# Subtraction, product and low half of the second softmax moved from GpSimd to VectorE for batches 1 to 7

## Chip, cores and metric

The kernel runs on one core of a Trainium2 chip. The core has five engines that run side by side and wait for each other by semaphores: TensorE (PE for its matmuls, PEld for its weight loads), VectorE (DVE), ScalarE (ACT), GpSimd (POOL) and SyncE (SP, which here issues the DMAs). The metric is device time in microseconds (us) of one execution. Lower is better.

## Reference

Two attentions with a softmax each, then two feed-forward layers. Shapes: batch B = 8, heads H = 8, sequence S = 576, head size 64, 32 packed rows; the layers have 4608 tokens, width 512 and inner width 2048. Weights come in 64-bit floats.

```python
def sm_attn(qq, kk, vv):
    s = scale * np.matmul(qq, kk.transpose(0, 1, 3, 2))
    s = s - np.max(s, axis=-1, keepdims=True)
    a = np.exp(s)
    a = a / (np.sum(a, axis=-1, keepdims=True) + 1e-09)
    return np.matmul(a, vv)
p_packed = sm_attn(p, k, v)             # first softmax, over 576
x = sm_attn(q, p_packed, p_packed)      # second softmax, over 32
x = x.transpose(0, 2, 1, 3).reshape(B * S, H * D)
h = x @ moe_w_in;  x = (h - np.tanh(h)) @ moe_w_out
h = x @ moe2_w_in; out = (h * np.cos(h)) @ moe2_w_out
```

## The kernel before, in words

**High and low halves.** A product is formed from a rounded high half and the rest, the low half: each operand t is split into h (ScalarE copies t to fp32r) and l = t - h, and three products h*h, l*h, h*l are summed in PSUM. The splits that this case touches are a2 (the second softmax's weights; L429 writes the high half, L430 the low half), g (L493, L498) and the layer's activations (gh on L561, gl on L565).

**Layer 1.** The last product of the second attention is never formed on its own: `gmat` multiplies the packed rows by the weights w1i (tile gp, L479), and `h1` (L517) multiplies the result g by the softmax weights a2. Work goes in 128 steps, `for n, (blk, s) in enumerate(steps)`. Each step makes one pair of h blocks with 12 matmuls of 128x288, works on it elementwise, and multiplies the activations of the step before last by w1o (`ymm1`, L578, 16 matmuls with gh and 8 with gl, into tile y). Per step the chain is: PE h; ACT t and u (L532, L533); DVE t, d, y, and the masked copy (L544, L545, L546, L550); ACT gh (L561); POOL gl (L565); PE y. L545 is the last that reads h from PSUM. On POOL a one-element memset (L556) of tile d stands ahead of gl, so that gl starts with L550 and not earlier.

**PSUM.** Pool `psh` has two tiles. All of these take turns in them: h of each step, the scores sc and s2, the transposes tp and pt, pp, and gp. A tile is taken again when its last reader is done: L545 for h, the second L498 for gp.

**Attention of batch b.** `attention(b, half)` queues 12 pieces, for two halves of the heads, into lists `early[n]` and `mid[n]`, which the steps n empty. For b >= 2 it starts at step at = 16 (b - 1); the second softmax of half 0 has s2 at step at+8, `s2m` at the end of at+8, `s2e` at the end of at+9, `s2n` at the end of at+10, `s2t` at the end of at+11, and `s2h` early in at+12, ahead of that step's L544. Half 1 is two steps later. So the ends of steps at+10 to at+14 and the starts of at+12 and at+14 hold the pieces in question; steps at+9, at+11, at+13 and at+15 hold gp and its two L498. The weights a2 are first used at step at+16. For b = 1 the pieces lie in steps 1 to 11, and its a2 are first used by h of step 8. Batch 0 comes ahead of the steps.

**Order.** From step 15 on the order of each engine's instructions is that of the code (`manual_schedule`). Steps 0 to 14 are ordered by the framework's scheduler, which places instructions by its own costs; there the engine of an instruction changes the order of others too.

After layer 1 comes layer 2 (from about 772 us), which uses none of the changed lines.

Of the kernel before, what the change touches and what calls it, by code (L numbers as in the profile page):

```python
# [78 lines left out]
def fused_kernel(ctx, tc, qT, kT, v, pT, w1i, w1o, w2i, w2o, ident, out):  # L79
    nc = tc.nc  # L80
# [241 lines left out]

    def attention(b, half, at=None, tsc=0, ttr=0, tpp=0, ts2=0):
        x = {}
        eng = nc.vector if b == 0 else nc.gpsimd

        def sc():
            k = ld.pop(("k", b, half))
# [645 lines left out]
    for x in LOADS.split():  # L974
# [6 lines left out]
        else:  # L981
            load0_qk(x[0], {"k": kT, "q": qT}[x[0]], int(x[1]))
    SCO, EX, RC, TR, PP, PX, S2, S2M, S2E, S2N, S2T, S2H = range(12)
    A0, A1 = (attention(0, half) for half in range(2))
    with tc.manual_schedule():
        for fn in (
# [20 lines left out]
    for b in range(1, B):  # L1007
        at = 16 * (b - 1)
        at_pair(at + (PACK1 if b == 1 else PACK), ppack, ppack2, b)
        for c in range(4):  # L1010
            at_pair(at + (G1 if b == 1 else G)[c], gmat, gsplit, b, c)
            if b > 1:
                mid[at + G[c] - 2].append(lambda c=c: load_w1(c))
        for half in range(2):
            attention(b, half, at, *(ATT1 if b == 1 else ATT)[half])
        lk0, lk1, lv0, lv1, lq0, lq1 = LOAD1 if b == 1 else LOAD
        mid[at - 4].append(lambda b=b: load_p(b))
        mid[at + lk0].append(lambda b=b: load_qk("k", kT, b, 0))
        mid[at + lk1].append(lambda b=b: load_qk("k", kT, b, 1))
        mid[at + lv0].append(lambda b=b: load_v(b, 0))  # L1020
        mid[at + lv1].append(lambda b=b: load_v(b, 1))
        mid[at + lq0].append(lambda b=b: load_qk("q", qT, b, 0))
        mid[at + lq1].append(lambda b=b: load_qk("q", qT, b, 1))
# [518 lines left out]
```

## Time and profile before

| | us |
|---|---|
| median of 3 runs (1494.94 to 1496.75) | 1496.19 |
| the profiled execution | 1494.03 |
| its span, first to last instruction | 1492.2 |
| PE, DVE, ACT, POOL busy | 1440.5, 1184.2, 1034.6, 383.8 |
| layer 1, steps 17 to 113, in the trace | about 153 to 700 |

The profiled execution is 2.2 us below the median of the three. Busy times of engines overlap each other; that an engine is busy doesn't say that anything waits for it.

### The profile page before, as it was taken

To read this page: it belongs to the slowest core of one execution; us is meant where nothing else is said; L and a number is where in the kernel's file an instruction comes from. 1 tells how busy PE (TensorE), PEld (TensorE's weight loads), DVE (VectorE), ACT (ScalarE), POOL (GpSimd) and SP (SyncE) were. 2 spreads that over 40 slices of the span, in tenths; PEclk is the share of its full clock that TensorE was granted. 3 is DMA by queue.
4 is the path that set the end of the run, shared out by engine and by line. 5 is a ranking of instruction groups with operands and counts; after the bars stand their busy time and mean duration, and the time that the engine had idled before them with its cause. 6 is when DMAs were issued, how large, how long until landed. Compare 5 with 4: busy or idle time off the path is not lost.

```text
span 1492.2 us, 29411 instructions
## 1 busy us (share of the span) xinstructions
PE 1440.5 (97%) x11296; PEld 1305.9 (88%) x11296; DVE 1184.2 (79%) x1562; ACT 1034.6 (69%) x1592; POOL 383.8 (26%) x356
## 2 busy tenths in 40 slices
PE   4789999999999999999999999999999999999998
PEld 2578999989998899988998888998889988998898
DVE  6998787777878788789976778886888688868874
ACT  5899767879788787977875656655665466636652
POOL 0353454554645455454550000000000000000000
PEclk8799999999999999999999999999999999999999
DMA  9642464646647474564669757776668766776656
GB/s 356 217 159 75 144 207 139 226 143 207 211 170 246 159 246 150 198 216 151 196 244 382 247 165 231 231 254 211 206 186 255 220 203 192 237 237 205 182 161 186
DMA packets 179980, 307.67 MB, mean 206 GB/s; under 512 B 14912, under 2 KB 110144, under 8 KB 179840
## 3 DMA queue, kind: packets, MB, share of 16 engines
q1 hardware_dynamic: 179840, 305.79, 62.8%
q8 instruction: 90, 1.47, 0.4%
q14 instruction: 50, 0.41, 0.1%
HBM read 238.35 MB, written 67.37 MB: 205 GB/s over the span
## 4 chain that ended last, share of the span: by engine, by line
PE 77%; ACT 8%; DVE 5%; issue 5%; POOL 3%; DMA 1%; SPq 0%; DVEq 0%; POOLq 0%; ACTq 0%
PE p L899 21%; PE y L578 17%; PE y L909 15%; PE h L517 9%; PE p L909 6%; PE h L639 3%; PE y L715 3%; POOL gl L565 2%; PE gp L479 2%; DVE y L550 1%; ACT u L533 1%; ACT st L175 1%; ACT st L170 1%; ACT y L539 1%; DVE y L546 1%
## 5 line engine op out<-in xcount | busy, mean ns | idle before, releaser
L899 PE MATMUL p<-b,hw 128*128 128x512 f32 x1302 | 310.4, 391 | 0.0
L578 PE MATMUL y<-gh,w1o 128*128 128x288 f32 x2048 | 305.3, 301 | 3.2 <-DVE ye L608 1.0
L578 PEld LDWEIGHTS y<-gh,w1o 128*128 128x128 f32 x2048 | 279.1, 189 | 31.1 <-issue 12.0
L899 PEld LDWEIGHTS p<-b,hw 128*128 128x128 f32 x1302 | 239.1, 188 | 47.0
L565 POOL TENSOR_TENSOR gl<-y,gh 128x576 fp32r<-128x576 f32 x127 | 245.7, 1935 | 22.4 <-ACT gh L561 22.4
L517 PE MATMUL h<-a,g 128*128 128x288 f32 x1536 | 228.8, 298 | 17.8 <-DVE d L545 7.6
L517 PEld LDWEIGHTS h<-a,g 128*128 128x128 f32 x1536 | 212.9, 190 | 21.7 <-ACT st L170 8.2
L532 ACT ACTIVATE t<-h 128x576 f32<-128x576 f32 x128 | 85.3, 667 | 122.9 <-PE h L517 122.8
L578 PE MATMUL y<-gl,w1o 128*128 128x288 f32 x1024 | 157.6, 296 | 5.5 <-POOL gl L565 5.2
L578 PEld LDWEIGHTS y<-gl,w1o 128*128 128x128 f32 x1024 | 142.7, 188 | 9.2 <-POOL gl L565 8.7
L550 DVE COPY_PREDICATED y<-k,t 128x576 f32<-128x576 int16 x128 | 132.4, 1035 | 9.9
L909 PE MATMUL y<-yw,yh 128*128 128x256 f32 x768 | 136.2, 279 | 0.2 <-DMA yw<-wod 0.2
L544 DVE TENSOR_TENSOR t<-h,t 128x576 f32<-128x576 f32 x128 | 95.2, 744 | 51.2 <-ACT u L533 50.7
L909 PEld LDWEIGHTS y<-yw,yh 128*128 128x128 f32 x768 | 117.6, 188 | 0.9 <-ACT o L920 0.4
L546 DVE SCALAR_TENSOR_TENSOR y<-y,d 128x576 f32<-128x576 f32 x128 | 104.0, 813 | 16.9 <-ACT y L539 10.4
L909 PE MATMUL y<-yw,yl 128*128 128x256 f32 x384 | 107.4, 280 | 0.0
L917 DVE TENSOR_TENSOR yl<-k,yh 128x1024 fp32r<-128x1024 f32 x72 | 87.1, 1220 | 23.4 <-ACT yh L920 22.9
L561 ACT ACTIVATE gh<-y 128x576 fp32r<-128x576 f32 x128 | 88.2, 689 | 9.9 <-DVE y L550 9.6
L545 DVE TENSOR_TENSOR d<-u,h 128x576 f32<-128x576 f32 x128 | 94.9, 742 | 0.0
L909 PE MATMUL y<-yw,gh 128*128 128x256 f32 x512 | 94.0, 280 | 0.0
L909 PE MATMUL p<-yw,yh 128*128 128x256 f32 x512 | 91.0, 279 | 0.0
L920 ACT ACTIVATE c<-p 128x512 f32<-128x512 f32 x96 | 56.9, 593 | 47.7 <-PE p L899 47.7
(166 smaller groups left out, 2609.1 us busy)
## 6 DMA issues: line engine op xcount, KB each, us to landing
yw<-wso SPq DMA_DIRECT2D x128, 256.0 KB, 3.0
hw<-wsi SPq DMA_DIRECT2D x124, 256.0 KB, 3.0
w1i<-w1d SPq DMA_DIRECT2D x48, 512.0 KB, 5.2
yw<-wod SPq DMA_DIRECT2D x96, 256.0 KB, 3.3
hw<-wid SPq DMA_DIRECT2D x93, 256.0 KB, 3.2
y<-ye SPq DMA_DIRECT2D x80, 144.0 KB, 1.9
st<-w1i SPq DMA_DIRECT2D x16, 512.0 KB, 8.4
v<-vv SPq DMA_DIRECT2D x16, 512.0 KB, 6.7
```

Source lines behind the costliest of these rows:

```text
L517: nc.tensor.matmul(out=h[:, x, 0:HB], lhsT=gw[b, f // 4, half][:, ga, c0:c0 + 128], rhs=a2[b, half][:, aa, HB * j:HB * j + HB], start=(n = ...
L532: nc.scalar.activation(out=st["t"], in_=h, func=AF.Tanh)
L544: lambda: nc.vector.tensor_tensor(out=t, in0=hs, in1=t, op=ALU.subtract),
L545: lambda: nc.vector.tensor_tensor(out=d, in0=u, in1=hs, op=ALU.mult),
L546: lambda: nc.vector.scalar_tensor_tensor(out=y, in0=y, scalar=PC0 - PC1 * PC1 / (4 * PC2), in1=d, op0=ALU.add, op1=ALU.mult,),
L550: lambda: nc.vector.copy_predicated(out=y, mask=k.bitcast(I16), data=t),
L561: nc.scalar.activation(out=st["gh"], in_=st["g"], func=AF.Copy)
L565: eng.tensor_tensor(out=st["gl"], in0=st["g"], in1=f32(st["gh"]), op=ALU.subtract)
L578: nc.tensor.matmul(out=yps[blk][d][:, 0:HB], lhsT=w1out[f][:, wh, 128 * d:128 * d + 128], rhs=st[gg][:, x, :], start=(s in first and x == ...
L899: nc.tensor.matmul(out=dst, lhsT=w[:, wi, 128 * j:128 * j + 128], rhs=b[j][bi], start=(first and n == 0), stop=(n == 5), skip_group_check= ...
L909: nc.tensor.matmul(out=dst[m // 2][:, 256 * (m % 2):256 * (m % 2) + 256], lhsT=src[:, 128 * m:128 * m + 128], rhs=w[:, wi, :], start=(firs ...
L917: nc.vector.tensor_tensor(out=out, in0=x, in1=y, op=op)
```

## The change

One line of `attention`: the engine of three instructions. Before, they ran on VectorE for batch 0 and on GpSimd for batches 1 to 7; now they run on VectorE for all.

```diff
     def attention(b, half, at=None, tsc=0, ttr=0, tpp=0, ts2=0):
         x = {}
-        eng = nc.vector if b == 0 else nc.gpsimd
+        eng = nc.vector
...
         def s2m():
...
             eng.tensor_tensor(
                 out=x["u3"], in0=x["u3"], in1=m.to_broadcast([128, NG, 32]), op=ALU.subtract
             )
...
         def s2n():
...
             eng.tensor_tensor(
                 out=x["u3"], in0=x["u3"], in1=r.to_broadcast([128, NG, 32]), op=ALU.mult
             )
...
         def s2h():
...
             eng.tensor_tensor(
                 out=t[:, 1, :], in0=x["ut"], in1=f32(t[:, 0, :]), op=ALU.subtract
             )
```

That is L407, L419 and L430, 128x576 each, in two halves of seven batches: 42 instructions. POOL keeps gl (L565), its memset, and the low halves of the weights (L232).

**Steps 42 and 43** (batch 3, as in batches 2 to 7), VectorE: the end of step 42 up to the first reads of h of step 43.

```order
 L417 TENSOR_SCALAR r<-r 128x18
 L418 RECIPROCAL r<-r 128x18
+L419 TENSOR_TENSOR u<-u,r 128x576
 L406 TENSOR_REDUCE m<-u 128x18
+L407 TENSOR_TENSOR u<-u,m 128x576
 L544 TENSOR_TENSOR t<-h,t 128x576
 L545 TENSOR_TENSOR d<-u,h 128x576
```

Two instructions now stand between L418 and L544.

**Step 44**, VectorE: the end of step 43 (g, then the transpose ut of half 0) and the start of step 44; `a_4070` is a2 of half 0 of batch 3.

```order
 L498 TENSOR_TENSOR g<-gp,g 128x512 x2
 L425 STREAM_TRANSPOSE ut<-u 128x576
+L430 TENSOR_TENSOR a_4070<-ut,a_4070 128x576
 L544 TENSOR_TENSOR t<-h,t 128x576
 L545 TENSOR_TENSOR d<-u,h 128x576
```

L430 reads what ScalarE's L429 writes, and L544 of step 44 now stands behind it. The end of step 44 (L418, L419, then L544 of step 45) has one more, and step 46 has L430 of half 1 ahead of its L544.

**The scheduled part, batch 1**, VectorE before: `a` isn't in these rows, since its low half is made on POOL; ut is that of half 1, and the L498 are those of the first gp of batch 1.

```order
118 L425 STREAM_TRANSPOSE ut<-u 128x576
119 L546 SCALAR_TENSOR_TENSOR y<-y,d 128x576
120 L208 SCALAR_TENSOR_TENSOR wt<-wt,st 128x512
121 L550 COPY_PREDICATED y<-k,t 128x576
122 L498 TENSOR_TENSOR g<-gp,g 128x512 x2
```

And now (`a_1145` is a2 of half 1 of batch 1):

```order
123 L498 TENSOR_TENSOR g<-gp,g 128x512
124 L550 COPY_PREDICATED y<-k,t 128x576
125 L498 TENSOR_TENSOR g<-gp,g 128x512
126 L425 STREAM_TRANSPOSE ut<-u 128x576
127 L208 SCALAR_TENSOR_TENSOR wt<-wt,st 128x512
128 L187 SCALAR_TENSOR_TENSOR st<-st 128x512
129 L208 SCALAR_TENSOR_TENSOR w1i<-w1i,st 128x512
130 L430 TENSOR_TENSOR a_1145<-ut,a_1145 128x576
```

The transpose has moved from ahead of the L498 to behind them, and three instructions of the weights' conversion stand between it and L430.

## Rows read from the trace of the kernel before

**Rows 1.** Busy us by stretch (PE, PEld, DVE, ACT, POOL), clock, DMA: scheduled part's end, then steps 17 to 113.
```profile
75.00:153.00 78.00, 69.91 (x642) 62.95 (x641) 69.69 (x95) 72.88 (x129) 36.37 (x37) 1.00 0.34 119
153.00:700.00 547.00, 539.41 (x5234) 500.17 (x5234) 438.47 (x672) 428.63 (x756) 285.21 (x259) 1.00 0.55 188
```

**Rows 2.** Waits of PE, 153 to 700 us: total us, times, longest.
```profile
PE h L517 <- DVE d L545: 2.3, 4, 0.7
PE y L578 <- POOL gl L565: 1.7, 3, 0.8
```

**Rows 3.** By source line: duration ns min/median/max, first and last start us.
```profile
L407 POOL TENSOR_TENSOR u<-u,m x14: 1153/1160/1687, 76.8 to 662.4; 128x576 f32<-128x576 f32 x14
L407 DVE TENSOR_TENSOR u<-u,m x2: 757/758/759, 20.6 to 22.9; 128x576 f32<-128x576 f32 x2
L417 DVE TENSOR_SCALAR r<-r x16: 158/618/627, 26.7 to 672.0; 128x18 f32<-128x18 f32 x16
L550 DVE COPY_PREDICATED y<-k,t x128: 795/830/2092, 46.8 to 769.5; 128x576 f32<-128x576 int16 x128
```

**Rows 4.** Timeline, steps 42 to 46: start us, us, instruction, [idle before, releaser].
```profile
301.57 0.70 DVE L406 TENSOR_REDUCE m<-u 128x18 f32<-128x576 f32 x1
302.25 0.76 DVE L544 TENSOR_TENSOR t<-h,t 128x576 f32<-128x576 f32 x1
302.92 0.74 DVE L545 TENSOR_TENSOR d<-u,h 128x576 f32<-128x576 f32 x1
...
305.23 1.76 PE L517 MATMUL h<-a,g 128*128 128x288 f32 x12
...
306.64 0.77 DVE L425 STREAM_TRANSPOSE ut<-u 128x576 f32<-128x576 f32 x1
308.11 0.69 ACT L429 ACTIVATE a<-ut 128x576 fp32r<-128x576 f32 x1
308.26 0.76 DVE L544 TENSOR_TENSOR t<-h,t 128x576 f32<-128x576 f32 x1 [0.85 <-ACT u L533]
...
309.98 0.96 DVE L546 SCALAR_TENSOR_TENSOR y<-y,d 128x576 f32<-128x576 f32 x1 [0.30 <-ACT y L539]
...
311.09 2.02 POOL L565 TENSOR_TENSOR gl<-y,gh 128x576 fp32r<-128x576 f32 x1
...
312.52 0.63 DVE L417 TENSOR_SCALAR r<-r 128x18 f32<-128x18 f32 x1
...
313.37 0.69 DVE L544 TENSOR_TENSOR t<-h,t 128x576 f32<-128x576 f32 x1
...
316.01 1.23 PE L517 MATMUL h<-a,g 128*128 128x288 f32 x8
```

**Rows 5.** Timeline, steps 78 to 80 of batch 5.
```profile
498.43 1.27 DVE L498 TENSOR_TENSOR g<-gp,g 128x512 fp32r<-128x512 f32 x2
...
500.15 1.76 PE L517 MATMUL h<-a,g 128*128 128x288 f32 x12
500.31 0.71 DVE L544 TENSOR_TENSOR t<-h,t 128x576 f32<-128x576 f32 x1
...
501.84 1.09 PE L479 MATMUL gp<-w1i,pt 64*32 64x256 f32 x32
...
509.15 0.72 PE L317 MATMUL sc<-k,pin 64*32 64x288 f32 x16 [0.76 <-PE h L517]
```

**Rows 6.** Timeline, step 30 of batch 2.
```profile
229.37 2.36 PE L578 MATMUL y<-gh,w1o 128*128 128x288 f32 x16 [1.05 <-DVE ye L608]
```

**Rows 7.** Timeline, scheduled part, around h of step 8, the first that needs a2 of batch 1.
```profile
92.90 1.82 POOL L430 TENSOR_TENSOR a<-ut,a 128x576 fp32r<-128x576 f32 x1
93.34 2.07 DVE L550 COPY_PREDICATED y<-k,t 128x576 f32<-128x576 int16 x1
...
99.50 0.40 PE L517 MATMUL h<-a,g 128*128 128x288 f32 x1 [2.13 <-ACT g L493]
...
102.09 1.19 PE L517 MATMUL h<-a,g 128*128 128x288 f32 x7 [0.17 <-POOL a L430]
```

## Prediction

> **What bounds the kernel now.** I read the busy times by stretch first [rows 1]. In steps 17 to 113, where 36 of the 42 moved pieces lie, PE is busy 539.4 of 547 us and VectorE 438.5: PE is the bound, and VectorE has 108 us idle. In the last 78 us of the scheduled part, where the six pieces of batch 1 lie, ScalarE is fullest (72.9 of 78), with PE and VectorE (69.9, 69.7) close behind. Then the waits of PE [rows 2]: from 153 to 700 us it waited 2.3 us for L545, four times, and 1.7 us for POOL's gl. So POOL costs PE next to nothing there, and taking work off it can give back 1.7 us at most. Then the timeline around one batch's pieces [rows 4], to see how late VectorE may be before PE waits. L545 of step 43 ends at 302.92 + 0.74 = 303.66, 1.41 us after its L544 began, and leaves its PSUM tile to h of step 44, which starts at 305.23: 1.57 us later. L544 of step 45 begins at 313.37, so its L545 ends at about 314.78 and h of step 46, which takes that tile, starts at 316.01: 1.23 us later. These two intervals, less some 0.1 us that a hand-over takes (my choice), are all the room there is.
>
> **The change, part by part.** A piece takes 0.76 us on VectorE (batch 0's, with POOL quiet) and took 1.16 on POOL [rows 3]. 36 pieces are 27 us, which would fit into 108 us of idle time if they stood where it is. They don't.
>
> *A shared resource.* L417 is a tiny instruction: 158 ns at the least, 618 at the median [rows 3]. In step 44 it starts at 312.52, beside gl (311.09 + 2.02 = 313.11), and ends at 313.15 [rows 4]: it was held until POOL was done. The Trainium skill, "SBUF — State Buffer", section "Who interferes with whom", has the rule: a Vector instruction with two SBUF inputs and a GpSimd instruction that reads SBUF exclude each other, and the later one waits for the whole of the earlier. By that rule alone each batch's first piece would cost its wait as well, and the sum below would be some 3 us higher. What the rows say of it: L407 of half 0, at the end of step at+8, comes beside a gl as that L417 does, and would be held some 0.5 us. I price it at nothing all the same: it is followed by an L544 that waits for ScalarE's u, as most of the L544 do, and by 1.5 us of room like that of step 43. If that cover were gone, it would cost up to 0.76 + 0.5 us in six batches, 8 us. The other five pieces of a batch come behind a finished gl, or while POOL waits, and run at 0.76.
>
> *Batch 3, step by step* [rows 4].
> - End of step 42: L419 and L407 in front of L544 of step 43, which started right behind L406 (301.57 + 0.70). It is late by 2 x 0.76 = 1.5 us. The room at step 44 is 1.57 - 0.1: PE loses 0 to 0.1.
> - Step 44: L425 is 1.5 us late too and ends at 308.9; ScalarE's L429 (0.69) waits for it instead of running at 308.11, and ends at 309.65; L430 follows, 0.76; L544 behind it starts at 310.4 instead of 308.26, 2.1 late. VectorE's idle 0.85 us ahead of that L544 is used up.
> - End of step 44: L546 had waited 0.30 us and taken 0.96 (beside POOL's L430; 0.76 otherwise), so the copy L550 and gl are 1.7 late, not 2.1. gl ends at 314.8, L417 is held until then, L418 and L419 follow: L544 of step 45 is 1.7 + 0.8 = 2.5 late, at 315.9, its L545 ends at 317.3, and h of step 46 starts at 317.4 instead of 316.01. **PE loses 1.4 us.**
> - Step 46: L430 of half 1 makes its L544 late again, but the next taker of that tile, gp of step 47, stands behind the 12 matmuls of another h. I take 0.
>
> Batches 4 and 6 repeat this: 3 x 1.4 = **4.2 us**.
>
> *Batches 5 and 7* have a long low half (128x1024, of the combined weights) at the end of steps 77 and 109. The two L498 behind it ended at 499.70 and end 2.2 us later (2.5 less the waits ahead of L546), at 501.9; h of step 79 takes their tile and started at 500.15, now 501.55: it loses 0.45 more. L425, L429 and L430 follow, so L544 of step 78 moves from 500.31 to about 501.85 + 0.77 + 0.69 + 0.76 + 0.1 = 504.1: 3.8 late. gp of step 79 takes that tile and started 0.1 us after its L545 (500.31 + 1.41 against 501.84), so PE is 3.8 late as well. At sc of step 80, where PE waited 0.76 us for a tile, 0.7 comes back [rows 5]. 3.1 each, **6.2 us**.
>
> *Batch 2.* PE already waits 1.05 us in step 30 for L608 [rows 6], four evacuations that stand behind L419, two L498 and L425 on VectorE. There is no room: they come as late as VectorE is at that point, 2.5 as in batch 3 and 0.4 more because VectorE waits less for u in step 28. **2.9 us**.
>
> *Batch 1, scheduled.* Most of h of step 8 started at 102.09, when POOL's L430 of half 1 was done [rows 7]. On VectorE this L430 now comes behind five other pieces and three conversions that stood elsewhere (the third pair of orders): 6 x 0.76 + 3 x 0.7 = 6.6 us more work ahead of it. Against this: L550 at 93.34 took 2.07 us beside POOL's L430 instead of 0.83 [rows 3, 7], 1.2 back; the piece itself is 0.7 shorter than its 1.46 on POOL (my estimate from the gap between 100.59, where ScalarE released it, and 102.05); and PE does about 0.9 us of y and gp ahead. That leaves 3.8. ScalarE, the fullest engine here, gets no work, so some of it comes back from later waits: I take **3 us**. Bounds: -2.1, if all of PE's idle time ahead of that h (2.13) went, and +6.6.
>
> *Sum.* 4.2 + 6.2 + 2.9 + 3 = 16.3. The profiled execution took 1494.0 and would take 1510.3; the median of the runs lies 2.2 above it, so about **1512 us**.
>
> **Rivals.** What a measurement of this kernel can tell from no change is about 0.2%, 3 us.
>
> *The room is enough (no change).* For it: VectorE is busy only 80% of the stretch, and the room is 1.57 and 1.23 us against pieces of 0.76. It would hold if the lateness did not pile up over steps 42 to 45, that is, if VectorE caught up in step 44. Against it: 0.85 + 0.30 + 0.2 us is all that it can catch up there, and three pieces are 2.3, with L429 in between. Batch 2 and the scheduled part would have to cancel too. 1496 us, within 3.
>
> *Faster: the softmax chain was POOL's.* "GPSIMD Engine Reference", Engine selection, in the Trainium skill, puts elementwise work on VectorE and calls GpSimd about two times slower with two inputs. The trace has 1.16 against 0.76 us [rows 3], 1.5 times. As a mechanism here: the chain to a2 of batch 1 gets 0.4 to 0.7 us shorter in each of its three pieces, h of step 8 no longer waits (2.13), and PE's waits for gl (1.7) go. That is 3.8 us, 1492. It decides if the last L425 of batch 1 is not held up behind the L498, and if nothing is lost in the steps at+13; the order shows the first to be otherwise.
>
> *VectorE becomes the bound around the pieces.* If each piece costs PE its whole 0.76 (27 us) and the scheduled part 6.6, it is 1494 + 34 + 2 = 1530. For it: three pieces in a row already leave no idle time. Against it: L407 of half 0 and L430 of half 1 have room.
>
> *The change does not do what it says:* excluded, since the order shows all 42 on VectorE.
>
> **How the numbers follow.** My forecast, slower by 6 to 25 us: 0.79. VectorE as the bound, above that: 0.05. A part of the terms covered, slower by 3 to 6 us: 0.04. Room enough: 0.07. Faster: 0.05. So slower 0.88, same 0.07, faster 0.05. The range: the steady term could be 1 to 1.5 times the three certain stalls (about 9 to 18 us), and the scheduled part -2 to 6.6; not all at one end: 1502 to 1521.
>
> **What would show it.** L407, L419, L430 on VectorE at 0.76, and at most the first of each batch longer. PE waiting for L545 some 1.4 us at the h of steps 46, 62 and 94; 1.4, 0.5 and 1.8 at the h, h and gp of steps 78 to 79, and the like at 110 to 111; the wait for L608 in step 30 grown from 1.05, together with that for L545 at its h, by 2.9. POOL some 50 us less busy and VectorE 25 to 30 more. h of step 8 some 3 to 4 us later. The prediction is wrong if L544 of step 45 is less than 1.2 us late, or if step 16 begins earlier than before, or if gl itself becomes late for PE.

## Result: slower by 1.1%, and the profile after

| | before | after |
|---|---|---|
| median of 5 runs each, us | 1496.01 (1494.94 to 1496.75) | 1511.79 (1510.35 to 1513.99) |
| ratio | 1 | 1.0113 [1.0103, 1.0124] |
| profiled execution, us (its span) | 1494.03 (1492.2) | 1513.38 (1511.6) |

The medians differ by 15.8 us, the two profiled executions by 19.4: that of before lies 2.0 under its median and that of after 1.6 above. Part of these 3.6 us is the clock of TensorE, told below; that it is all of them isn't shown.

Busy time of the changed kernel, from the page:

```profile
PE 1445.8 (96%) x11296; PEld 1309.1 (87%) x11296; DVE 1213.2 (80%) x1604; ACT 1038.0 (69%) x1592; POOL 330.5 (22%) x314
```

Busy us by stretch, the end of the scheduled part and steps 17 to 113, with the clock granted to PE after the engines (compare [rows 1]):

```profile
75.00:158.00 83.00, 71.02 (x639) 63.68 (x638) 73.68 (x100) 73.24 (x129) 28.63 (x31) 0.98 0.31 110
158.00:720.00 562.00, 544.31 (x5238) 503.06 (x5237) 463.58 (x709) 432.29 (x756) 240.10 (x223) 1.00 0.54 183
```

Steps 17 to 113 take about 562 us instead of 547 (14.8 us more up to step 120, by the starts of h). GpSimd has lost 45 us of work there and VectorE has gained 25, but VectorE still has 98 us idle. So these 15 us are no lack of time on VectorE. The waits of PE in that stretch (total us, times, longest; compare [rows 2]):

```profile
PE h L517 <- DVE d L545: 8.5, 12, 1.0
PE gp L479 <- issue: 3.3, 2, 1.6
PE y L578 <- DVE ye L608: 2.1, 1, 2.1
PE sc L317 <- PE h L517: 2.1, 4, 0.6
PE y L578 <- POOL gl L565: 0.7, 1, 0.7
```

PE waits for L545 three times as often. The two "issue" waits at gp are also waits for a PSUM tile that L545 had not left (below). The moved pieces themselves, by source line (duration ns min/median/max; compare [rows 3]):

```profile
L407 DVE TENSOR_TENSOR u<-u,m x16: 745/760/1200, 20.9 to 680.1; 128x576 f32<-128x576 f32 x16
L419 DVE TENSOR_TENSOR u<-u,r x16: 739/758/760, 27.4 to 692.1; 128x576 f32<-128x576 f32 x16
L430 DVE TENSOR_TENSOR a<-ut,a x16: 734/758/762, 31.7 to 700.9; 128x576 fp32r<-128x576 f32 x16
```

They take 0.76 us at the median, as forecast; some L407 take up to 1.20. Batch 3, timeline of steps 43 to 45 (compare [rows 4]; h of step 42 begins 10.03 us later than before):

```profile
313.18 0.76 DVE L407 TENSOR_TENSOR u<-u,m 128x576 f32<-128x576 f32 x1
313.85 0.75 DVE L544 TENSOR_TENSOR t<-h,t 128x576 f32<-128x576 f32 x1
...
318.13 0.77 DVE L425 STREAM_TRANSPOSE ut<-u 128x576 f32<-128x576 f32 x1
318.93 0.69 ACT L429 ACTIVATE a<-ut 128x576 fp32r<-128x576 f32 x1 [0.45 <-DVE ut L425]
...
319.64 0.76 DVE L430 TENSOR_TENSOR a<-ut,a 128x576 fp32r<-128x576 f32 x1 [0.75 <-ACT a L429]
...
320.32 0.75 DVE L544 TENSOR_TENSOR t<-h,t 128x576 f32<-128x576 f32 x1
...
325.82 0.75 DVE L544 TENSOR_TENSOR t<-h,t 128x576 f32<-128x576 f32 x1
```

Take 10.03 us off each L544 and compare with 302.25, 308.26 and 313.37: they are 1.6, 2.0 and 2.4 us late (forecast 1.5, 2.1, 2.5). Between them L429 waits for the late L425, and L430 waits 0.75 us for L429 while L544 stands behind it.

Batch 5, steps 78 and 79 (compare [rows 5]; h of step 76 begins 13.3 us later than before):

```profile
515.06 1.84 PE L517 MATMUL h<-a,g 128*128 128x288 f32 x12 [0.31 <-DVE g L498]
515.64 0.69 ACT L429 ACTIVATE a<-ut 128x576 fp32r<-128x576 f32 x1 [2.82 <-DVE ut L425]
516.35 0.76 DVE L430 TENSOR_TENSOR a<-ut,a 128x576 fp32r<-128x576 f32 x1 [0.75 <-ACT a L429]
517.03 0.75 DVE L544 TENSOR_TENSOR t<-h,t 128x576 f32<-128x576 f32 x1
...
518.54 1.10 PE L479 MATMUL gp<-w1i,pt 64*32 64x256 f32 x32 [1.64 <-issue]
```

gp starts 0.1 us after the end of the L545 behind that L544: that is what "issue" hides. It is 16.7 us later than before, so 3.4 us were lost since step 76 (forecast 0.45 + 1.4 + 1.8 = 3.65 up to there, of which 0.7 comes back).

### The profile page after: what moved, and what is told of

Same layout as the page of the kernel before. It is cut to its first block, busy times and chain, and to the rows that moved or that the text cites. A ratio compares the mean times of both kernels' runs of the same rounds, so it can differ in the third digit from the quotient of the medians.

```text
span 1511.6 us, 29391 instructions
## 1 busy us (share of the span) xinstructions
PE 1445.8 (96%) x11296; PEld 1309.1 (87%) x11296; DVE 1213.2 (80%) x1604; ACT 1038.0 (69%) x1592; POOL 330.5 (22%) x314
## 4 chain that ended last, share of the span: by engine, by line
PE 77%; DVE 8%; ACT 7%; issue 5%; POOL 2%; DMA 1%; SPq 0%; DVEq 0%; ACTq 0%; POOLq 0%
PE p L899 20%; PE y L578 17%; PE y L909 15%; PE h L517 10%; PE p L909 6%; PE h L639 3%; PE y L715 3%; DVE y L550 2%; PE gp L479 1%; POOL gl L565 1%; DVE t L544 1%; DVE d L545 1%; ACT u L533 1%; ACT st L175 1%; DVE y L546 1%
## 5 line engine op out<-in xcount | busy, mean ns | idle before, releaser
L565 POOL TENSOR_TENSOR gl<-y,gh 128x576 fp32r<-128x576 f32 x127 | 246.4, 1940 | 30.5 <-ACT gh L561 30.2
L517 PEld LDWEIGHTS h<-a,g 128*128 128x128 f32 x1536 | 213.5, 190 | 33.1 <-PE y L578 13.9
L550 DVE COPY_PREDICATED y<-k,t 128x576 f32<-128x576 int16 x128 | 131.0, 1023 | 9.9 <-ACT k L542 0.2
L544 DVE TENSOR_TENSOR t<-h,t 128x576 f32<-128x576 f32 x128 | 95.6, 747 | 37.6 <-ACT u L533 36.8
L546 DVE SCALAR_TENSOR_TENSOR y<-y,d 128x576 f32<-128x576 f32 x128 | 99.8, 780 | 15.8 <-ACT y L539 8.5
L561 ACT ACTIVATE gh<-y 128x576 fp32r<-128x576 f32 x128 | 88.1, 688 | 15.1 <-DVE y L550 14.8
L545 DVE TENSOR_TENSOR d<-u,h 128x576 f32<-128x576 f32 x128 | 94.9, 742 | 0.0
L556 POOL MEMSET d<- 128x1 f32 x127 | 12.6, 99 | 363.7 <-DVE y L546 353.2
L539 ACT ACTIVATE y<-u 128x576 f32<-128x576 f32 x128 | 87.4, 683 | 6.5 <-POOL gl L565 6.0
```

The costliest lines, as they stand in the source:

```text
L517: nc.tensor.matmul(out=h[:, x, 0:HB], lhsT=gw[b, f // 4, half][:, ga, c0:c0 + 128], rhs=a2[b, half][:, aa, HB * j:HB * j + HB], start=(n = ...
L539: nc.scalar.activation(out=y, in_=u, func=AF.Square, scale=PC2 ** 0.5, bias=PC1 / (2 * PC2 ** 0.5))
L544: lambda: nc.vector.tensor_tensor(out=t, in0=hs, in1=t, op=ALU.subtract),
L545: lambda: nc.vector.tensor_tensor(out=d, in0=u, in1=hs, op=ALU.mult),
L546: lambda: nc.vector.scalar_tensor_tensor(out=y, in0=y, scalar=PC0 - PC1 * PC1 / (4 * PC2), in1=d, op0=ALU.add, op1=ALU.mult,),
L550: lambda: nc.vector.copy_predicated(out=y, mask=k.bitcast(I16), data=t),
```

## Experiments

Each kernel ran on one chip beside the kernel before, not all on the same chip; "ratio" is against that kernel there, with its 95% interval. The table shows how many us each stretch of the program grew against the profiled execution of before, from the starts of the first weight load of h in steps 8, 17, 34, 50, 66, 82, 98 and 120.

| kernel | ratio | batch 1 | 2 | 3 | 4 | 5 | 6 | 7 |
|---|---|---|---|---|---|---|---|---|
| changed | 1.0113 [1.0103, 1.0124] | 5.5 | 4.6 | 1.4 | 1.5 | 3.2 | 1.4 | 2.8 |
| changed, again | 1.0110 [1.0096, 1.0124] | 6.6 | 2.9 | 1.4 | 1.5 | 3.2 | 1.4 | 3.0 |
| batch 1 only | 1.0026 [1.0017, 1.0035] | 4.1 | 0.0 | 0.0 | 0.0 | 0.0 | 0.0 | 0.0 |
| batches 2 to 7 | 1.0120 [1.0106, 1.0133] | 0.9 | 2.9 | 2.3 | 1.5 | 3.2 | 1.5 | 3.2 |
| low half only | 1.0040 [1.0028, 1.0053] | 1.0 | 0.9 | 0.0 | 0.0 | 1.4 | 0.1 | 1.2 |
| subtraction, product | 1.0076 [1.0063, 1.0089] | 0.0 | 3.6 | 1.4 | 0.6 | 1.5 | 0.6 | 2.0 |
| low half late | 1.0075 [1.0063, 1.0088] | 1.1 | 4.1 | 0.8 | 0.8 | 2.6 | 0.8 | 2.8 |
| first subtraction | 1.0000 [0.9992, 1.0009] | 1.0 | 0.0 | 0.0 | 0.0 | 0.2 | 0.6 | 0.0 |
| changed, L608 first | 1.0114 [1.0099, 1.0130] | 4.1 | 6.6 | 1.4 | 1.4 | 3.1 | 1.8 | 2.9 |
| the same, stores kept | 1.0104 [1.0089, 1.0120] | 6.5 | 3.7 | 1.4 | 1.4 | 3.1 | 1.8 | 3.0 |
| before, L608 first | 1.0002 [0.9993, 1.0011] | 1.0 | 0.1 | 0.0 | 0.0 | 0.1 | 0.0 | 0.0 |
| low half twice | 1.0088 [1.0074, 1.0102] | 0.8 | 1.6 | 1.3 | 1.3 | 4.3 | 1.3 | 3.9 |
| batch 1: four pieces | 1.0009 [1.0000, 1.0018] | 4.2 | 0.1 | 0.0 | 0.0 | 0.1 | 0.0 | 0.0 |

**Batch 1 only.**

```diff
-        eng = nc.vector
+        eng = nc.vector if b < 2 else nc.gpsimd
```

> The six pieces of batch 1 alone (with those of batch 0, which were there before) on VectorE; GpSimd keeps the 36 of batches 2 to 7. Theory (late turns of the two-tile PSUM pool, and a longer chain to the low half of batch 1's a2): step 17 begins 5.5 us later than before, as in the changed kernel, nothing is added after it, and the h of steps 46, 62, 94 and the gp of steps 79 and 111 wait as before; median 1500 to 1502. Rival 1 (each piece costs the same share of the 15.8 us): 6 of 42 pieces, 2.3 us, 1498.3. Rival 2 (the steps written by hand hold the whole loss): 1496.

Step 17 begins 3.7 us later (it grew 4.1 from step 8 on, which began 0.4 early), and nothing is added behind it. The median, 1498.57, is under the 1500 to 1502 that I expected. It is 3.7 us above before's 1494.82 and so above both rivals, the nearer one only just (its interval is 2.5 to 5.2, that rival at 2.3). It stays 1.8 us under the 5.5 of the changed kernel, with the same order on PE. Most of that is the clock: behind the wait for L429, from 104.86 us to the start of the last matmuls of h, 4 matmuls of h, 12 of gp and 5 of y took 3.5 us there, at 0.50 from about 105 us on, and 2.1 in this kernel at 1.00. This kernel's clock fell as well, from 99.0 to 102.4 us, but ahead of a wait for L429 (1.12 us).

**Batches 2 to 7.**

```diff
-        eng = nc.vector
+        eng = nc.gpsimd if b == 1 else nc.vector
```

> All 36 pieces of batches 2 to 7 on VectorE, those of batch 1 on GpSimd as before. Theory: steps 0 to 16 as before; then batch 2 +4.3, batches 3, 4 and 6 +1.4 each, 5 and 7 +2.8 each as in the changed kernel, 14 us in the trace by step 127; median 1506 to 1509. The two parts add up: this and the kernel with batch 1 alone together make the 15.8 us. Rival (the parts hide each other, or GpSimd's relief in batch 1 pays for some of it): the sum of the two differs from 15.8 by more than 2 us.

Batch by batch it loses what the changed kernel loses, batch 2 even the forecast 2.9. The median is 1512.16, 3 us above what was expected, and by medians the two parts sum to 0.26 + 1.20 = 1.46%, where the whole has 1.10 to 1.13; by the profiled spans they sum to 3.1 + 15.4 = 18.5 us against 19.4. So GpSimd's relief pays for nothing: a sum that misses the whole by more than 2 us was the rival's sign, and by medians it does (21.1 against 15.8), but upwards, where that rival has it smaller. These 0.35% are more than the intervals explain, and stay open. Batch 3 lost 0.9 more than batches 4 and 6; the last section has the cause.

**Low half only; subtraction and product only** (batches 2 to 7; batch 1 on GpSimd).

```diff
-        eng = nc.vector
+        eng, low = (nc.vector if b == 0 else nc.gpsimd), (nc.gpsimd if b == 1 else nc.vector)
...
-            eng.tensor_tensor(
+            low.tensor_tensor(
                 out=t[:, 1, :], in0=x["ut"], in1=f32(t[:, 0, :]), op=ALU.subtract
```

The second kernel has the two engines exchanged.

> Of batches 2 to 7 only the low half of a2 (L430) on VectorE, 12 pieces; the subtraction and the product stay on GpSimd, and so does all of batch 1. Theory (lateness piles up from three pieces ahead of one turn of the PSUM pool): L430 makes L544 of step 44 1.3 us late, L544 of step 45 at most 0.8, which is under the 1.2 of room, so the h of steps 46, 62 and 94 wait as before; in batches 5 and 7 gp of steps 79 and 111 comes 1.9 late and 0.7 is given back, 1.2 each; batch 2 some 0.8; together about 3 us, median 1498 to 1500. Rival (each piece costs its share, 36 pieces some 11 us): 12 pieces 3.7 us with a third of the 1.2 us wait, 0.4, at each of the h of steps 46, 62 and 94.

> Of batches 2 to 7 the subtraction and the product (L407, L419) on VectorE, 24 pieces; the low half (L430) stays on GpSimd, and so does all of batch 1. Theory: L544 of step 43 is 1.5 us late as in the changed kernel and h of step 44 waits 0.25; L425 is 1.5 late, but nothing on VectorE waits for ScalarE's L429 any more, so L544 of step 44 is only 0.7 late and L544 of step 45 1.2 to 1.6: h of step 46 waits 0 to 0.4. Batches 3, 4 and 6 some 0.4 each, 5 and 7 0.6 each, batch 2 some 1.5: about 4 us, median 1498 to 1501. Rival (each piece costs its share): 24 of 36 pieces, some 7.5 us, 1503 to 1504, with 0.8 of the 1.2 at the h of step 46.

By whole times the two halves add up (0.40 and 0.76 against 1.20%), which is what the rival says, and both are slower than I expected. The single steps say otherwise. In batch 4 the h of step 62 loses nothing with the low half alone and 0.38 us with the other two (by the weight loads), where the rival has 0.4 and 0.8, and the changed kernel lost 1.23. What made the second kernel's whole time long are batch 2 (3.6 where I had 1.5; its clock was at 0.50 from 232.6 to 236.0 us, behind the wait for L608), batch 3, with the same 0.9 as above, and batches 5 and 7, which lost 1.5 and 2.0 where I had 0.6.

**Low half late.** All 36 pieces stay on VectorE; L430 goes behind L550.

```diff
-            eng.tensor_tensor(
-                out=t[:, 1, :], in0=x["ut"], in1=f32(t[:, 0, :]), op=ALU.subtract
-            )
+            def lo():
+                eng.tensor_tensor(
+                    out=t[:, 1, :], in0=x["ut"], in1=f32(t[:, 0, :]), op=ALU.subtract
+                )
+            if b > 1:
+                mid[at + ts2 + 5 - half].append(lo)
+            else:
+                lo()
```

> All 36 pieces of batches 2 to 7 on VectorE as in the kernel with these alone, and as many instructions; only L430 is moved: behind L550 at the end of a step (half 0 one step after its high half, half 1 in the same step) instead of ahead of L544. Theory (what costs is lateness piled up ahead of one L545, not the work): L544 of step 44 is 0.7 us late instead of 2.0, L544 of step 45 1.2 to 1.6 instead of 2.4, so h of steps 46, 62 and 94 waits 0 to 0.4 instead of 1.2; h of step 44 0.25 as before. In batches 5 and 7 L430 of half 0 now comes behind the long L789 and L498 and ahead of L544 of step 78, so gp loses about as much as in the kernel with all on VectorE (1.2), and they keep 2 to 3 each. Batch 2 loses 1.5 to 2.5. Together 7 to 9 us instead of 14 in the trace; median 1501 to 1505. Rival (VectorE's load decides, or each piece has its price): 14 us as in the kernel with these alone, 1509 to 1512.

The same work in another order costs 0.75% instead of 1.20 (on different chips, each against the kernel before): the rival falls. Batches 3, 4 and 6 lose 0.8 instead of 1.5, with 0.16 at the h of step 62. Batch 2 lost 4.1, with the clock at 0.50 from 233.7 to 237.1 us; the median, 1507.82, is 3 us over the expected.

**Low half twice.** The kernel with the low half alone, each L430 written twice, with the same values.

> The kernel with the low half of a2 alone on VectorE (batches 2 to 7), and each L430 done twice with the same result: 12 more instructions of 0.75 us. Theory (a threshold, the room of 1.2 us): L544 of step 44 is 2.1 us late instead of 1.3, L544 of step 45 1.5 instead of 0.8, and the h of steps 46, 62 and 94, which did not wait, now wait 0.3 to 0.5; the gp of steps 79 and 111 have no room and lose the whole 0.75 more, as do the L608 of batch 2; together 3 to 4 us over the kernel with one L430, median 1503 to 1505. Rival (each piece has its price of some 0.4 us wherever it stands): 5 us more, spread over all six batches alike, 0.8 each; rival 2 (amount of work without a threshold): 0.75 more at every one of the h that follow.

The h of steps 46, 62 and 94, which lost nothing, lose 0.58 each: the threshold is there. But the doubled L430 of half 1, which I had left out, costs 0.7 more at the next step, and at the gp of steps 79 and 111 3.3 and 2.7 are lost where one L430 lost 1.2 and 0.9 and 0.75 more was expected. The wait of gp in step 79 grew by 0.8 as expected (1.64 to 2.43 us); the rest is the clock, at 0.50 from 509.1 to 512.5 us, where the 32 matmuls took 1.96 us instead of 1.09, and again from 696.8 us behind gp of step 111. So batches 2 to 7 lose 10.4 us more in the trace (13.9 against 3.5) and 7 by medians, not 3 to 4. Both rivals fall by the single steps, the loss of nothing at one L430 and of 0.58 at two; the whole times alone would not have told (the first rival has 5).

These kernels side by side, in batch 4: h of step 61, L544 of step 61 and h of step 62, from the timelines (edits move line numbers by 1 or 5). First the kernel before:

```profile
399.68 1.76 PE L517 MATMUL h<-a,g 128*128 128x288 f32 x12
403.04 0.69 DVE L544 TENSOR_TENSOR t<-h,t 128x576 f32<-128x576 f32 x1
405.69 1.76 PE L517 MATMUL h<-a,g 128*128 128x288 f32 x12
```

The changed kernel:

```profile
411.36 1.76 PE L517 MATMUL h<-a,g 128*128 128x288 f32 x12
416.94 0.75 DVE L544 TENSOR_TENSOR t<-h,t 128x576 f32<-128x576 f32 x1
418.50 1.83 PE L517 MATMUL h<-a,g 128*128 128x288 f32 x12 [0.97 <-DVE d L545]
```

Low half only:

```profile
402.14 1.76 PE L517 MATMUL h<-a,g 128*128 128x288 f32 x12
406.35 0.69 DVE L544 TENSOR_TENSOR t<-h,t 128x576 f32<-128x576 f32 x1
408.15 1.76 PE L517 MATMUL h<-a,g 128*128 128x288 f32 x12
```

Subtraction and product:

```profile
405.78 1.76 PE L517 MATMUL h<-a,g 128*128 128x288 f32 x12
410.51 0.75 DVE L544 TENSOR_TENSOR t<-h,t 128x576 f32<-128x576 f32 x1
412.07 1.84 PE L517 MATMUL h<-a,g 128*128 128x288 f32 x12
```

Low half late (L549 is L544):

```profile
406.29 1.76 PE L522 MATMUL h<-a,g 128*128 128x288 f32 x12
410.80 0.75 DVE L549 TENSOR_TENSOR t<-h,t 128x576 f32<-128x576 f32 x1
412.35 1.84 PE L522 MATMUL h<-a,g 128*128 128x288 f32 x12
```

Low half twice (L545 is L544):

```profile
402.32 1.76 PE L518 MATMUL h<-a,g 128*128 128x288 f32 x12
407.31 0.70 DVE L545 TENSOR_TENSOR t<-h,t 128x576 f32<-128x576 f32 x1
408.81 1.83 PE L518 MATMUL h<-a,g 128*128 128x288 f32 x12 [0.21 <-DVE d L546]
```

Measure each from its own h of step 61. In before L544 comes 3.36 us behind it and the next h 6.01.

| kernel | L544 late by | h of step 62 late by | difference |
|---|---|---|---|
| low half only | 0.85 | 0.00 | (under the room) |
| low half late | 1.15 | 0.05 | 1.10 |
| subtraction, product | 1.37 | 0.28 | 1.09 |
| low half twice | 1.63 | 0.48 | 1.15 |
| changed | 2.22 | 1.13 | 1.09 |

Whatever the pieces are, PE loses nothing up to 1.1 us of lateness and, in the four kernels beyond that, all that goes beyond it. That is the room that the prediction read from [rows 4], 1.23 less 0.1. (By the weight loads the losses are some 0.1 greater; a waiting h also runs 1.83 instead of 1.76.)

**First subtraction** (L407 of half 0 in batches 2 to 7, which was priced at nothing).

```diff
-            eng.tensor_tensor(
+            (nc.vector if b > 1 and half == 0 else eng).tensor_tensor(
                 out=x["u3"], in0=x["u3"], in1=m.to_broadcast([128, NG, 32]), op=ALU.subtract
```

> The kernel before with one piece of each of batches 2 to 7 on VectorE: L407 of half 0, the one that was priced at nothing. Theory: it stands beside gl and is held for some 0.4 us, so takes 1.2, but L544 behind it waits for ScalarE or has 1.5 us of room; no h and no y starts later, the cumulated shift by step 127 is under 0.3 us; median 1495 to 1496.5 (as before). Rival (by the hold each such piece costs PE its wait and itself, 1.2 us): 6 x 1.2, 7 us, 1502. Rival 2 (by the share of a piece, 16 us over 42): 2.3 us, 1497.5.

```profile
L407 DVE TENSOR_TENSOR u<-u,m x8: 757/1198/1206, 20.4 to 650.2; 128x576 f32<-128x576 f32 x8
```

Six of the eight are held beside gl and take 1.2 us, and PE loses nothing by it: ratio 1.0000. The 0.6 in batch 6 are at step 96, not at a moved piece (the last section has it). The Trainium skill, "SBUF — State Buffer", section "Who interferes with whom", says that the two exclude each other; the 1.2 us agree. The price of nothing holds as well, since the hold falls into room.

**L608 first** (of the changed kernel). At the end of a block y is finished and L608 put ahead of the step's other late work.

```diff
+        if len(hist) == 2 and hist[0][0] < NP and hist[0][1] == NSTEP - 1:
+            hb, hs, hst = hist.pop(0)
+            ymm1(hb, hs, hst)
+            yevac1(hb)
         for fn in mid[n]:
             fn()
```

> The changed kernel with the four evacuations L608 at the end of a block put ahead of that step's other VectorE work (in step 29 ahead of two L498 and L425, 2.0 us). Theory (batch 2's loss is mainly that y of step 30 waits for L608 behind L498 and L425, and that the clock may fall in that wait): PE's wait for L608 in step 30 goes from 2.1 to under 0.5, no fall of the clock there, and batch 2 costs 1 to 2 us against the kernel before instead of 4.3; the rest as in the changed kernel; median 2 to 3.5 us under the changed kernel of the same chip. Rival (L498 and L425, now 1.5 us later, cost as much elsewhere): no difference, and PE waits for L545 or L498 at the h or gp of steps 31 and 32 instead.

PE's wait for L608 in step 30 went from 2.14 to 0.30 us, but the next gp waited instead:

```profile
242.80 0.67 PE L479 MATMUL gp<-w1i,pt 64*32 64x256 f32 x16 [2.15 <-DMA w1i<-w1d]
...
244.24 1.11 PE L479 MATMUL gp<-w1i,pt 64*32 64x256 f32 x16 [0.77 <-DMA w1i<-w1d]
```

The four stores behind L608 had moved with it, ahead of the load of gp's weights in SP's queue. The median is 1514.02, 1.2 us above the changed kernel's 1512.78 on that chip, where 2 to 3.5 less was expected. So the rival was right on the whole, by a way that it had not named.

**The same with the stores kept in place**, on the changed kernel and on the one before.

> The changed kernel with the four evacuations L608 ahead of that step's other VectorE work as in the trial before, but with their stores left at their old place in SP's queue, so that the load of the weights for gp of step 31 is not behind them. Theory: PE's wait for L608 in step 30 is 0.3 us instead of 2.1, gp of step 31 no longer waits for its load (2.15 and 0.77 us there in the trial before), and batch 2 costs 1 to 2 us against the kernel before; no fall of TensorE's clock in step 30; median 1.5 to 3 us under the changed kernel (1.0095 to 1.0105 of before). Rival (the two L498 and L425 that now stand 1.5 us later cost as much): PE waits at the h or gp of steps 31 and 32 for L498 or L545, and batch 2 costs 3 us or more.

> The kernel before (GpSimd keeps its pieces) with the same move: the four L608 ahead of that step's other VectorE work, their stores where they were. Theory: PE's wait of 1.05 us for L608 in step 30 goes and nothing takes its place, 1 us in the trace; median 1494.5 to 1496, at the edge of what can be told. Rival: the wait turns up at gp of step 31 or h of step 32, no change in the trace.

In both the wait for L608 goes, but for 0.3 us in the changed kernel (on the kernel before 1.3 us are won at step 30), and both give it back in part or whole: 1.3 us at step 26, where the edit also put another L608 ahead of two L498, whose tile the scores s waited for. In the changed kernel, gp of step 31 waits 0.75 us besides. On before the sum is nothing; on the changed kernel batch 2 keeps 3.7, more than the 2.9 that it lost without the move in the profile whose clock stayed at 1.00 there, and the ratio, 1.0104, can't be told from 1.0110. In these trials an instruction that leaves a PSUM tile, moved ahead, made another one late. No version here beats the kernel before.

**Batch 1: four pieces.** The kernel before with subtraction and product of batch 1 on VectorE, its low half on GpSimd.

> The kernel before with the subtraction and the product of batch 1 (four pieces) on VectorE and its low half on GpSimd; the framework orders the first 15 steps anew and puts two L498 ahead of the last L425 again. Theory (h of step 8 comes late because L430 of half 1 stands behind L425, L498 and three conversions on VectorE): with L430 on GpSimd, which starts it as soon as ScalarE's L429 is done, the last matmuls of h of step 8 start 2 to 4 us later than before instead of 4.5 to 6.3, and step 17 begins 1 to 3 us later instead of 3.7; median 1496.5 to 1499. Rival (the late L425, behind the L498 that the framework put ahead of it, is all of it): step 17 as late as with all six pieces, 3.7 us or more. Rival 2 (the low half alone was the cost): step 17 as before.

Step 17 begins 3.4 us later than before, so the theory's 1 to 3 is missed. L425, L429 and L430 of half 1, first in the kernel before (its L430 is on GpSimd, 100.59 to 102.05):

```profile
96.82 0.78 DVE L425 STREAM_TRANSPOSE ut<-u 128x576 f32<-128x576 f32 x1
...
99.83 0.68 ACT L429 ACTIVATE a<-ut 128x576 fp32r<-128x576 f32 x1
```

Batch 1 only (all six pieces):

```profile
102.05 0.77 DVE L425 STREAM_TRANSPOSE ut<-u 128x576 f32<-128x576 f32 x1
...
103.77 0.67 ACT L429 ACTIVATE a<-ut 128x576 fp32r<-128x576 f32 x1
...
105.75 0.74 DVE L430 TENSOR_TENSOR a<-ut,a 128x576 fp32r<-128x576 f32 x1
```

Four pieces:

```profile
101.76 0.78 DVE L425 STREAM_TRANSPOSE ut<-u 128x576 f32<-128x576 f32 x1
...
103.47 0.78 ACT L429 ACTIVATE a<-ut 128x576 fp32r<-128x576 f32 x1
...
104.35 1.87 POOL L430 TENSOR_TENSOR a<-ut,a 128x576 fp32r<-128x576 f32 x1
```

The last seven matmuls of h of step 8 start at 106.55 in both new kernels (102.09 before), so the reason that I gave, L430 queued on VectorE, does not hold: that queue costs 1.3 us, but on GpSimd L430 takes 1.87 us instead of 0.74. What both share is L425, 5 us late, and L429, 3.6 to 3.9 us late; L429 also starts 0.9 us after the end of L425, because conversions now stand ahead of it on ScalarE, where it came right behind L493 before. This fits the rival, nearly in its size too (3.4 against 3.7); no run put L425 back. That the growth is the same (4.2 against 4.1) says less, since this profile has its clock at 0.50 from 104 to 111 us. And the median is only 1.5 us above before's (0.0 to 2.7), less than with six (2.5 to 5.2). How much of the term is L425 stays open.

**The changed kernel again.**

> The changed kernel once more, on the same chip as the three below. Theory: in its first profile two of the terms held a second cost that is no part of the late VectorE. TensorE's granted clock fell to 0.50 after it had stood waiting, for 105 to 108 us (step 8) and for 239 to 241.4 us (step 30), some 1.7 and 1.5 us; with the same waits it stayed at 1.00 in step 30 of the kernel with batches 2 to 7 alone, and fell at a place that cost less in step 8 of the kernel with batch 1 alone. So in this profile step 17 begins 3.7 us later than before without that fall and 5.5 with it, and batch 2 costs 3.0 without and 4.4 with it; the h of steps 46, 62 and 94 lose 1.2 as before. Median 1508 to 1512. Rival (both excesses belong to the order of the work): 5.5 and 4.3 again, with the clock at 1.00 all along.

Batch 2 now costs 2.9, with the clock at 1.00 in step 30; batch 1 costs 6.6, with the clock at 0.50 from about 100 to 110 us. So the first is what I expected and forecast (the median, 1512.78, is just above the range expected), and the second is not separated from the clock by these runs.

## Why the prediction was right

The forecast was 1512 us and the median is 1511.79. The mechanism, lateness ahead of a PSUM tile's release, is borne out; that the medians agree this closely is in part luck. The forecast terms sum to 16.3 us, and the terms of the two profiles to 20.4 and 20.0, while the medians differ by 15.8 and, in the second run, 16.8.

- **Batches 3, 4 and 6:** forecast 1.4 us each, measured 1.4 to 1.5 in both profiles of the changed kernel, by the chain of lateness that the steps gave (1.6, 2.0, 2.4 against 1.5, 2.1, 2.5). One detail was off: 0.25 of it falls at h of step 44, where 0 to 0.1 was given, and 1.2 at h of step 46. The table of lateness shows the room, 1.1 us, and the kernel with the low half late shows that order decides, not the amount of work alone.
- **Batches 5 and 7:** forecast 3.1 each, measured 3.2 and 2.8 to 3.0, at the h, the h and the gp named.
- **Batch 2:** forecast 2.9; 2.9 again and in the kernel with batches 2 to 7 alone, 4.6 in the first profile. The wait for L608 grew from 1.05 to 2.14 and that for L545 at h of step 30 was 0.95. That is 2.0 (2.3 by the starts of the weight loads), and the other 0.55 fell at h of step 28, where none was forecast, so 2.9 is right as a sum and not in each part. Of what the first profile has beyond it, some 1.4 us are the slower matmuls of y at the lower clock.
- **Batch 1:** forecast 3, and here the step failed in size and in reason. It grew 5.5 and 6.6 in the changed kernel, 4.1 alone. "Some of it comes back from later waits" did not happen: nothing came back after step 9 but what the order moved within the scheduled part. The last seven matmuls of h of step 8 came 6.3 us later in the first profile and 4.5 alone, where 3 to 4 was forecast. And the pieces and "three conversions that stood elsewhere" ahead of L430 are not what decides, since L430 on GpSimd lets h start no earlier; the late L425 and L429 ahead of it are left as the likelier cause, not shown by a run of their own. Part of the excess over 4.1 is the clock.
- **First subtraction at nothing:** shown by its own run. The prediction took the held L417 as its sign that L407 would be held; L417 reads one tile and L407 two, and it is this run that shows L407 itself held, 1.2 us for 0.76.
- **Against the profiled execution:** the sum gave 1510.3 for a profile and 1513.4 came. The kernel before had no fall of the clock at step 8 in its profile; five of seven other kernels with its order there had one, and 0.9 to 1.1 us of growth in that stretch (the two without one grew 0.0 and 0.75). So its profile was probably a lucky one, and the difference of the medians, 15.8, is nearer to 16.3 than that of the profiles, 19.4.
- **Rivals.** Room enough: each half of the change nearly fits into it (0.0 and 0.6 in batch 4), the whole does not (1.5). VectorE as the bound: it stays idle for 98 of 562 us, and the kernel with the low half late does the same work for over a third less loss.

## What to carry to other kernels

Moving work to an engine with idle time costs nothing only where the room at each hand-over behind it holds all that stands ahead of it in one turn: read the room at the releasing instruction (here 1.1 us at L545), add up the lateness over the steps that share it, and price only what goes beyond. Work placed ahead of such a release, and above all work that waits for a third engine there, costs more than the same work behind it. And a wait of PE may cost more than its length: look at the granted clock of the stretch behind it, in more than one profile, before a term is called mis-sized.

## What the hardware showed that I had not expected

**The clock after a wait.** Busy us by stretch in step 30 of the changed kernel (PE first; the clock stands after POOL), then of the kernel with batches 2 to 7 alone:

```profile
235.60:237.60 2.00, 0.00 (x0) 0.00 (x0) 2.00 (x5) 1.54 (x3) 0.95 (x1) 1.00 0.00 0
...
239.00:241.40 2.40, 2.40 (x11) 2.40 (x11) 2.30 (x4) 0.60 (x2) 0.00 (x0) 0.50 0.88 257
```

And the kernel with batches 2 to 7 alone:

```profile
230.20:232.30 2.10, 0.00 (x0) 0.01 (x1) 2.10 (x5) 1.62 (x3) 1.02 (x1) 1.00 0.00 0
232.30:234.50 2.20, 2.18 (x16) 2.20 (x17) 2.20 (x5) 1.97 (x4) 0.00 (x0) 1.00 0.59 201
```

PE stood idle for 2.14 and 2.15 us, with the clock at 1.00. Behind it the clock fell to 0.50 (1.2 GHz) in the one and stayed at 1.00 (2.4 GHz) in the other. The 16 matmuls of y took 3.73 us instead of 2.37. The same wait cost 1.4 us more or not, from one profile to the next; behind the 1.05 us wait of the kernel before [rows 6] no fall was seen. In step 8 of the changed kernel it fell right behind a wait of 1.15 us that came after waits of 2.23 and 1.33, so the length of one wait doesn't tell.

**Which of two comes first.** L550 usually starts 0.1 us behind L546 and takes 0.83, with gl beside it at 2.0. In step 45 of the kernel with batches 2 to 7 alone it started late:

```profile
314.86 0.76 DVE L546 SCALAR_TENSOR_TENSOR y<-y,d 128x576 f32<-128x576 f32 x1
...
315.77 1.42 POOL L565 TENSOR_TENSOR gl<-y,gh 128x576 fp32r<-128x576 f32 x1
...
316.08 1.81 DVE L550 COPY_PREDICATED y<-k,t 128x576 f32<-128x576 int16 x1 [0.46 <-ACT t L532]
```

gl was first, ran in 1.42 us, and L550 was held to 1.81. h of step 46 lost 2.10 us there instead of 1.22. It was the same in step 45 of the kernel with subtraction and product (L550 at 1.80, 1.25 lost instead of 0.38), and L550 at 597.37 took 1.78 in the kernel with the first subtraction, ahead of the 0.6 us lost in its batch 6. Single profiles differ by such events by 0.6 to 0.9 us in a batch that has one.
